# A two-resolution attention and its feed-forward layer: batch 0's mask and sums on TensorE, batch 1 in halves

## The chip, the core and the metric

The kernel runs on one NeuronCore of a Trainium2 chip. The core has five engines with instruction queues of their own: TensorE (PE, matmuls, with its weight loads shown as PEld), VectorE (DVE), ScalarE (ACT), GpSimd (POOL) and SyncE (SP), which here only issues transfers. TensorE writes to PSUM, eight banks of 128 x 512 fp32; DVE and ACT bring results from there to SBUF, POOL works in SBUF alone. Transfers are issued by SP and by POOL and run on 16 DMA engines. The metric is the time on the device in microseconds (us). Before the change it is 363.93, the median of 3 runs (363.8 to 364.75).

## The reference

For 8 batches of 8 heads with 576 tokens of 64 elements, attention is computed twice and added: on q, k, v averaged over groups of 4 tokens (144 x 144 scores per head), its result repeated 4 times; and on the full tokens, where a token sees only those less than 4 positions away. The result, 4608 tokens x 512, goes through a feed-forward layer with ELU.

```python
factor = 4
scale = 1.0 / np.sqrt(D)
q_d = q.reshape(B, H, Sd, factor, D).mean(axis=3)      # k_d, v_d alike
out_up = np.repeat(sm_attn(q_d, k_d, v_d), factor, axis=2)
mask = np.abs(pos[:, None] - pos[None, :]) < factor
scores = np.where(mask, scale * np.matmul(q, k.transpose(0, 1, 3, 2)), -1000000000.0)
attn = softmax(scores)
x = (out_up + np.matmul(attn, v)).transpose(0, 2, 1, 3).reshape(4608, 512)
h = x @ w_in                                           # 512 -> 2048
g = np.where(h > 0.0, h, np.exp(np.minimum(h, 0.0)) - 1.0)
return g @ w_out                                       # 2048 -> 512
```

## The kernel before, in words

**Attention.** A batch has four pairs of heads; a pair fills TensorE's 128 rows. For each pair q and k are loaded (96 tokens on the partitions, six columns of them), cast to fp16 (`cast`), transposed on TensorE by a matmul with an identity (`transposes`; the averages over four tokens come from a second matmul with the matrix BY6 for batches 0 and 1, whose tokens are loaded in another order, or from extra columns of ONE for the rest) and evicted to SBUF (`evq`, `evk`). `scores` multiplies, for each of six blocks of 96 queries, the 102 keys that can be in reach, and the averaged tokens beside them; ACT takes the exponential of each head; DVE multiplies the local part by the 0/1 tile MASK (line 644). `denominators` sums exponentials on TensorE (four pairs in four column groups of the array at once), DVE takes reciprocals, and these are spread over the head's 64 partitions: for batches 0 and 1 by TensorE with the constant SEL and a copy by ACT (`spr`, `evr`), for the others by two transfers through DRAM. `pool_v` averages v. `outputs` multiplies exponentials and v, DVE normalises (`normalize`, line 771, tile xn, three buffers), and an addition of the local and the repeated part writes the block of x, transposed, that the feed-forward layer reads (line 787, tile xt).

**Feed-forward.** Nine blocks of 512 tokens ("stages" 0 to 8). In a stage `mm1` does 16 groups of four matmuls with w_in (line 804), ACT takes exp, DVE min and the ELU's sum (lines 812 and 815); `mm2` does four results of 16 matmuls with w_out (line 827), each in four groups; ACT copies and SP stores. A batch has 576 tokens, so batch 0 fills the first block and 64 tokens of the second. Attention of later batches runs between the groups of earlier stages.

**What sets the order.** Nothing is issued in program order. Every step is an `Op` with an engine, an estimated length, a rank and the buffers it needs. `Plan.run` simulates engines and transfers with these estimates and, whenever an engine is free, starts the ready step of lowest rank; `emit` issues the steps in the order found, which each engine then keeps. Ranks are worked out from the numbers in PARAM. Before the first stage the planner fills PE's gaps up to a time FILL with matmuls on zeros (line 329, 221 of them, 17.3 us busy). Gates hold transfers back: `LGATE` makes loads of batch 1 wait for a named step by a small DVE memset into their buffer (line 879), `WGATE` orders weight transfers behind POOL's casts. Since SP issues in order, a gated load holds all that stand behind it. w_in comes in five transfers (bounds in WIC), w_out in four, all on POOL's queue.

**Constants.** DVE fills nine tiles (`fills`), POOL cuts the diagonals and bands with selects (`diagonals`, `masks`); transposes wait for the first, masks and denominators for both.

**Batch 0's end.** Each of four pairs is normalised; per pair, 512 of the 576 tokens are added for the first block by POOL (288) and DVE (224), and 64 by POOL for the second.

```python
    c_a = op("POOL", 2.0, -60, diagonals, after=[o_fill], name="diag")
    c_b = op("POOL", 1.9, -59, masks, after=[o_fill], name="masks")
            eng = "DVE" if b == 0 and g == 1 and t == 0 else "POOL"
        op("PE", 0.863, r, lambda: go(range(DMC)), reads=[x], writes=[h], after=[wi_ops[fc]], name=f"mm1_{t}_{fc}")
            need = [o for o in gt.writers if int(o.name.split("_")[1]) < 4 * part + 4]
            o.pre.add(wo_ops[part])
```

Of the kernel before, what the change touches and what calls it, by code (L numbers as in the profile page):

```python
# [31 lines left out]
DEN_GROUPS = {0: ((0, 1), (2, 3))}  # L32
# [3 lines left out]
LGATE = (None, "mask01", "mask02", "mask03", "recip02", "xn00", "xn01", "xn02", "xn03", "elu0_0", "elu0_2", "elu0_4", "elu0_8")  # L36
BY_PE = (0, 1)
V0 = ("DVE", "ACT")
WIC = (0, 256, 512, 1024, 1536, 2048)
# [30 lines left out]
class Plan:  # L70


    LAT = {"PE": 0.22, "ACT": 0.09, "DVE": 0.09, "POOL": 0.15}
# [60 lines left out]
    def run(self):  # L134
# [24 lines left out]
        busy = dict.fromkeys(ready, 0.0)  # L159
        events, now, order, lanes = [], 0.0, [], []  # L160
# [13 lines left out]
        while n < len(self.ops):  # L174
            for e, todo in ready.items():
# [36 lines left out]
                if o.nbytes:  # L212
                    if e == "SP":
                        lanes.append(o)
                    queues[e].append([o, o.nbytes / o.rate])
                    done = None
                else:
                    done = now + dur + (self.LAT[e] if o.lag is None else o.lag)
# [7 lines left out]
            then = min(events[0][0] if events else 1e9, land() if now >= 2.0 else max(land(), 2.0))  # L226
            if now >= 2.0:
                for e, f in shares().items():
                    x = queues[e][0]
                    x[1] -= (then - now) * f  # L230
                    if x[1] < 1e-6:
                        queues[e].pop(0)
                        heapq.heappush(events, (then + 1.5, x[0].i, x[0]))
            now = then
            self.filling = now < self.fill
            while events and events[0][0] <= now + 1e-9:
                _, _, o = heapq.heappop(events)
                if o is None:
                    continue
# [14 lines left out]
    def emit(self):  # L254
        for o in self.order:
# [8 lines left out]
PARAM = dict(M0=30, P=36.77, LAG=1.06, LEAD=53.49, GAP=7.69, SC=3.9, DEN=33.04, OUT=1.4, OUTG=1.98,  # L264
             LOAD=23.14, VLOAD=27.91, VCAST=36.99, warm=3.4, FILL=27.63, WI=-27.58, WO=38.12, WOG=2.24,
             OVER=1.0, LEAD1=57.82, GAP1=5.57, OUT1=32, VLOAD1=41.43, LOAD1=28.31, CC=-45.43, tv0=-26.96,
             C0=-7.99, SC0=2.71, OUTA=-25.9, OUTB=-21.42, DEN0=3.42, DENB=-28.86, SPA=-26.1, SPB=-20.87,
             V0=-46.5, G0=1, G1=2, G2=3, G3=3, G4=3, G5=8, G6=3, G7=13, G8=13, L0=2, L1=6, L2=0, L3=8,
             L4=0, LAG0=1.07, QG=2.08)
# [3 lines left out]
def kernel(  # L273
# [62 lines left out]
    def const(name, shape):  # L336
# [9 lines left out]
        "GAP": const("GAP", [QB, 41]),  # L346
        "SEL": const("SEL", [128, 640]),
# [4 lines left out]

    def fills():
        for t, x in (("ONE", 0.0), ("BY6", 0.25), ("VR", 0.25), ("MASK", 1.0), ("IND", 0.0), ("FIRST", 1.0), ("GAP", 0.0)):
            nc.vector.memset(C[t][:], x)  # L355
        nc.vector.memset(C["ONE"][:, QB:], 0.25)
        nc.vector.memset(C["VR"][:, 24:], 0.0)
        nc.vector.memset(C["IND"][:, 9:10], 1.0)
        nc.vector.memset(C["FIRST"][:, 1:10], 0.0)
        for i in range(3):  # L360
            nc.vector.memset(C["GAP"][32 * i : 32 * i + 24, 9:10], 1.0)
        for t in T["kt"]:
            nc.vector.memset(t[:, 0:3], 0.0)
            nc.vector.memset(t[:, S + 3 : S + 6], 0.0)
        for t in KD:
            nc.vector.memset(t[:], 0.0)

    o_fill = op("DVE", 1.6, -98, fills, name="fills")
# [9 lines left out]
    def diagonals():  # L378
        band(C["BY6"][:], [[1, NB], [-4, SD]], 6, 0, 3)
        nc.gpsimd.affine_select(  # L380
            out=C["ONE"][:, 0:QB], in_=C["ONE"][:, 0:QB], pattern=[[-1, QB]], compare_op=AB.not_equal, fill=1.0,
# [482 lines left out]
    for i in range(9):  # L864
        weights(i)
# [63 lines left out]
```

## Time and profile before

| what | before |
|---|---|
| median of 3 runs | 363.93 us (363.8 to 364.75) |
| the profiled execution: its time, its span | 364.62 us, 362.9 us |
| mean clock granted to TensorE | 0.984 |
| busy: PE, DVE, ACT, POOL | 347.5, 224.4, 211.5, 144.0 us |
| matmuls with w_in, with w_out (busy) | 141.2, 140.3 us |
| matmuls on zeros | 221, 17.3 us |
| moved by DMA | 48.89 MB, 135 GB/s in the mean |

Busy times say how long instructions of an engine were under way; a PE that is busy may run pipelined matmuls or small ones. What counts is where PE stands while something else ends last, and at which clock it runs. In the page's slices each digit is the busy share of a fortieth of the span, 9.07 us. In timelines the columns are start, length, engine, line, operation, output and inputs; in brackets the idle time before and what released the engine. A table of stretches gives for each engine its busy time and its number of instructions.

### The profile page before, as it was taken

How to read it: one execution, taken by the hardware profiler on the slowest of the kernel's cores; microseconds unless marked ns; L12 is line 12 of the kernel's file. 1: busy time of each engine (PE TensorE's matmuls, PEld its weight loads, DVE VectorE, ACT ScalarE, POOL GpSimd, SP SyncE). 2: the span in 40 equal slices, each digit the busy share in tenths (PEclk: the TensorE clock that was granted, in tenths of full speed). 3: DMA queues.
4: the chain of work that ended last, by engine and by line, in shares of the span. 5: the costliest groups of instructions: out<-in, count | busy, mean ns of one | idle time of the engine just before them, and what ended most of it. 6: DMA issues, size and time to landing. Idle time of an engine off the chain costs nothing.

```text
span 362.9 us, 8968 instructions
## 1 busy us (share of the span) xinstructions
PE 347.5 (96%) x3677; PEld 189.3 (52%) x3677; DVE 224.4 (62%) x410; ACT 211.5 (58%) x364; POOL 144.0 (40%) x226
## 2 busy tenths in 40 slices
PE   8995999999998998999999999999999999999995
PEld 7984554455454554554555455555554444444442
DVE  3658598336885597557755865398547667765510
ACT  2643696469865677557855785488557415544411
POOL 7645554277274544570557055634330160000000
PEclk9998799899999999999999999999999999999999
DMA  8999999999979799479746975103001311010021
GB/s 218 216 157 225 258 199 191 202 201 235 234 168 222 193 181 220 93 157 214 155 94 153 218 149 99 61 35 83 31 30 60 87 48 40 0 58 33 29 77 68
DMA packets 114366, 48.89 MB, mean 135 GB/s; under 512 B 100662, under 2 KB 108662, under 8 KB 114326
## 3 DMA queue, kind: packets, MB, share of 16 engines
q1 hardware_dynamic: 108038, 39.49, 52.3%
q0 software_dynamic: 6288, 8.84, 13.3%
q8 instruction: 28, 0.46, 0.6%
q14 instruction: 12, 0.10, 0.1%
HBM read 42.86 MB, written 9.66 MB: 145 GB/s over the span
## 4 chain that ended last, share of the span: by engine, by line
PE 78%; DVE 9%; ACT 6%; issue 2%; DMA 2%; POOL 2%; ACTq 0%; DVEq 0%; POOLq 0%
PE bank L827 32%; PE bank L804 27%; PE bank L548 4%; PE bank L620 3%; PE bank L748 3%; DVE e L812 3%; PE bank L329 3%; ACT e L810 2%; DVE gt L815 2%; PE bank L665 2%; ACT ex L637 2%; DVE ex L644 2%; DMA rcb<-rd 1%; PE bank L540 1%; PE bank L756 1%
## 5 line engine op out<-in xcount | busy, mean ns | idle before, releaser
L804 PE MATMUL bank<-xt,WI 128*128 128x512 f16 x576 | 141.2, 382 | 1.6 <-DVE gt L815 1.4
L827 PE MATMUL bank<-WO,gt 128*128 128x512 f16 x576 | 140.3, 381 | 1.9 <-DVE gt L815 1.9
L810 ACT ACTIVATE e<-bank 128x512 f16<-128x512 f32 x144 | 85.1, 603 | 49.1 <-PE bank L804 27.2
L815 DVE SCALAR_TENSOR_TENSOR gt<-bank,e 128x512 f16<-128x512 f32 x144 | 97.8, 688 | 4.9
L827 PEld LDWEIGHTS <-gt 128*128 128x128 f16 x576 | 54.0, 98 | 64.4 <-DVE gt L815 2.6
L804 PEld LDWEIGHTS <-WI 128*128 128x128 f16 x576 | 53.1, 98 | 64.0 <-issue 6.3
L812 DVE TENSOR_SCALAR e<-e 128x512 f16<-128x512 f16 x144 | 55.4, 386 | 39.6 <-ACT e L810 38.8
L516 POOL CAST c<-ld 96x768 f16<-96x768 f32 x60 | 50.6, 861 | 50.5 <-issue 25.7
L637 ACT ACTIVATE ex<-bank 102x864 f16<-102x864 f32 x64 | 53.4, 887 | 23.7 <-PE bank L628 23.5
L787 POOL TENSOR_TENSOR xt<-xn 128x288 f16<-128x288 f16 (+8 forms) x92 | 44.4, 514 | 54.1 <-DVE xn L771 54.0
L644 DVE TENSOR_TENSOR ex<-ex,MASK 102x1152 f16<-102x1152 f16 x32 | 28.6, 895 | 41.5 <-ACT ex L637 41.4
L842 ACT COPY os<-bank 128x512 f32<-128x512 f32 x36 | 21.3, 590 | 46.4 <-PE bank L827 43.4
L771 DVE TENSOR_TENSOR xn<-bank,rcb 128x720 f16<-128x720 f32 x32 | 27.8, 901 | 25.6 <-PE bank L756 23.8
L473 POOL CAST v<-v 102x768 f16<-102x768 f32 x32 | 27.5, 887 | 0.3 <-DMA v<-in_v_dram 0.3
L548 PEld LDWEIGHTS <-c 96*128 96x128 f16 x288 | 18.1, 97 | 8.0 <-issue 0.4
L563 ACT CAST qt<-bank 128x720 f16<-128x720 f32 x24 | 18.3, 761 | 4.2 <-PE bank L548 3.7
L548 PE MATMUL bank<-ONE,c 96*128 96x120 f16 x288 | 20.6, 216 | 0.0
L719 POOL DMA_DIRECT2D rd<-rc x6 | 3.5, 578 | 41.3 <-DVE rc L692 19.7
L329 PE MATMUL bank<-zero 128*128 128x128 f16 x221 | 17.3, 240 | 1.8 <-DVE ONE L355 1.1
L620 PEld LDWEIGHTS <-kt 64*102 64x102 f16 x384 | 11.7, 125 | 12.6 <-ACT e L810 4.7
L575 ACT CAST kt<-bank 128x576 f16<-128x576 f32 x24 | 15.6, 651 | 1.2 <-ACT qt L563 1.2
L329 PEld LDWEIGHTS <-zero 128*128 128x128 f16 x221 | 15.1, 109 | 2.4 <-DVE zero L332 1.1
(67 smaller groups left out, 228.6 us busy)
## 6 DMA issues: line engine op xcount, KB each, us to landing
ld<-in_q_dram SPq DMA_DIRECT2D x32, 288.0 KB, 5.2
ld<-in_k_dram SPq DMA_DIRECT2D x32, 288.0 KB, 5.4
out_dram<-os SPq DMA_DIRECT2D x36, 256.0 KB, 2.0
v<-in_v_dram SPq DMA_DIRECT2D x13, 672.0 KB, 8.8
rcb<-rd POOLq DMA_DIRECT2D x12, 360.0 KB, 5.6
WO<-in_moe_w_out_dram POOLq DMA_DIRECT2D x4, 512.0 KB, 9.1
WI<-in_moe_w_in_dram POOLq DMA_DIRECT2D x3, 512.0 KB, 11.3
v<-in_v_dram SPq DMA_DIRECT2D x3, 336.0 KB, 8.6
```

Source lines behind the costliest of these rows:

```text
L329: nc.tensor.matmul(PS[:, 7, 384:512], zero[:, 0:128], zero[:, 128:256], start=True, stop=True)
L516: f(out=at(y)[:], in_=at(x)[:].rearrange("p e c d -> p c e d"))
L548: nc.tensor.matmul(o, t[:, c, :, :], C["ONE"][:], start=True, stop=True)
L637: lambda e=e: nc.scalar.activation(out=at(x)[:, e], in_=two(sc[e], 0, KW, 0, HB + SD), func=AF.Exp, scale=SCALE),
L644: nc.vector.tensor_tensor(out=a, in0=a, in1=mk, op=AB.mult)
L771: lambda: nc.vector.tensor_tensor(out=at(w)[:], in0=two(z, 0, 128, 0, GW), in1=at(y)[:, j], op=AB.mult),
L787: (nc.vector if eng == "DVE" else nc.gpsimd).tensor_tensor(out=at(xt(t))[:, j, o : o + n - a], in0=ln, in1=gn, op=AB.add)
L804: nc.tensor.matmul(one(h, 0, 128, 0, TBLK), WI[:, dc, 128 * fc : 128 * fc + 128], at(x)[:, dc, :], start=(dc == 0), stop=(dc == DMC - 1),)
L810: op("ACT", 0.55, r, lambda: nc.scalar.activation(out=at(e)[:], in_=one(h, 0, 128, 0, TBLK), func=AF.Exp), reads=[h], writes=[e], name=f"e ...
L812: op("DVE", 0.42, r, lambda: nc.vector.tensor_scalar(out=at(e)[:], in0=at(e)[:], scalar1=1.0, scalar2=-1.0, op0=AB.min, op1=AB.add), reads ...
L815: op("DVE", 0.64, r, lambda: nc.vector.scalar_tensor_tensor(out=at(gt)[:, fc, :], in0=one(h, 0, 128, 0, TBLK), scalar=0.0, op0=AB.max, in1 ...
L827: nc.tensor.matmul(one(z, 0, 128, 0, DM), at(gt)[:, fc, 128 * tt : 128 * tt + 128], WO[:, fc, :], start=(fc == 0), stop=(fc == FCN - 1),)
```

## The change

Batch 0 changes in two ways, batch 1 in one, and the planner's estimates and numbers all change.

- **Mask.** For batch 0 the product with MASK on DVE goes. TensorE first writes a tile NEG (0 where a key is in reach, -30000 elsewhere) into the score banks, by four matmuls with an identity EYE per pair, and the scores accumulate on it.
- **Sum.** For batch 0's first block the additions by POOL and DVE go. TensorE adds the local and the repeated part with EYE in one PSUM bank per pair (four matmuls), and ACT copies the bank to xt.
- **Constants.** Each is made by a step of its own, in another order; MASK is cut for one block by POOL and copied to the others by DVE; the identity is EYE.
- **Batch 1.** Denominators and spreads are done for two pairs at a time, and the pooled v becomes a step of its own.
- **w_in** comes in four transfers of 512 columns; weight gates and load gates are other steps.
- **Engines of batch 0's casts and evictions** are set one by one: all four q casts and the third k cast on POOL, the other k casts on DVE; evictions of q on DVE but for the second pair, those of k on ACT for the first two pairs and on DVE for the others.
- The planner models transfers with other rates, starts and landings. Its order has 140 matmuls on zeros.

```diff
+MASK_BY_PE = (0,)
-DEN_GROUPS = {0: ((0, 1), (2, 3))}
+DEN_GROUPS = {0: ((0, 1), (2, 3)), 1: ((0, 1), (2, 3))}
...
-LGATE = (None, "mask01", "mask02", "mask03", "recip02", "xn00", "xn01", "xn02", "xn03", "elu0_0", "elu0_2", "elu0_4", "elu0_8")
+LGATE = (None, "recip00", "evv00", "recip00", "recip02", "xn00", "xn01", "xn02", "xn03", "elu0_0", "elu0_2", "elu0_4", "elu0_8")
-WIC = (0, 256, 512, 1024, 1536, 2048)
+WIC = (0, 512, 1024, 1536, 2048)
...
-             V0=-46.5, G0=1, G1=2, G2=3, G3=3, G4=3, G5=8, G6=3, G7=13, G8=13, L0=2, L1=6, L2=0, L3=8,
-             L4=0, LAG0=1.07, QG=2.08)
+             V0=-44.04, G0=1, G1=0, G2=4, G3=3, G4=12, G5=10, G6=13, G7=13, G8=13, L0=0, L1=1, L2=5, L3=10,
+             L4=2, LAG0=1.13, BY4=-31.8, TV1=4.97, C1=-16.44, e_x0=1, e_x1=1, e_x2=1, e_x3=1, e_cq0=1, e_cq1=1,
+             e_cq2=1, e_cq3=1, e_ck0=0, e_ck1=0, e_ck2=1, e_ck3=0, e_q0=0, e_q1=1, e_q2=0, e_q3=0, e_k0=1,
+             e_k1=1, e_k2=0, e_k3=0, QG=1.2)
...
+    c_six = op("POOL", 2.2, -60, sixths, name="sixths")
+    c_eye = op("POOL", 0.25, -59, eye, after=[o_clear], name="eye")
+    c_m1 = op("POOL", 0.75, -58, mask1, after=[o_clear], name="mask1")
+    c_m6 = op("DVE", 0.55, -57, mask6, after=[c_m1], name="mask6")
+    c_mask = op("POOL", 0.25, -56, edge, after=[c_m6], name="edge")
+    c_neg = op("DVE", 0.45, -54, lambda: nc.vector.tensor_scalar(
+        out=C["NEG"][:], in0=C["MASK"][:], scalar1=-1.0, scalar2=30000.0, op0=AB.add, op1=AB.mult), after=[c_mask], name="neg")
...
+            if hide:
+                for e in range(2):
+                    for g in range(2):
+                        nc.tensor.matmul(
+                            PS[0:KW, sc[e].slot[0] + g, 0:HB], C["EYE"][0:KW, 0:KW],
+                            C["NEG"][:, 3 * g : 3 * g + 3].rearrange("p c u -> p (c u)"), start=True, stop=False,
+                        )
...
-        op("DVE", 0.76, r + 0.6, mask, reads=[x], writes=[x], after=[c_b], name=f"mask{b}{j}")
+        if b not in MASK_BY_PE:
+            op("DVE", 0.76, r + 0.6, mask, reads=[x], writes=[x], after=[c_mask], name=f"mask{b}{j}")
...
+    def add_by_pe(j, r, w):
+        z, x = Buf("one"), xt(0)
+        def go():
+            for g, a, n in ((0, 0, HB), (1, HB, TBLK)):
+                ln = at(w)[:, g, 0 : n - a]
+                gn = at(w)[:, g, HB : HB + (n - a) // 4]
+                gn = bass.AP(tensor=gn.tensor, offset=gn.offset, ap=list(gn.ap) + [[0, 4]])
+                nc.tensor.matmul(one(z, 0, 128, a, n), C["EYE"][:], ln, start=True, stop=False)
+                nc.tensor.matmul(one(z, 0, 128, a, n), C["EYE"][:], gn, start=False, stop=True)
+        op("PE", 0.45, r + 0.3, go, reads=[w], writes=[z], after=[c_eye], name=f"sum0{j}")
+        eng = ("DVE", "ACT")[PARAM[f"e_x{j}"]]
...
+        if b == 0:
+            add_by_pe(j, r, w)
+            cuts = [TBLK, S]
...
-        if b == 0:
+        if b in DEN_GROUPS:
             yv, zv, w, tv = pool_v(b)
```

## The prediction, made before the changed kernel ran

> **What bounds the kernel now.** I read the slices of the page first, then the chain that ended last, then the engines stretch by stretch, then DVE's and PE's timelines around the places where PE stands. In the slices PE is 8 or 9 tenths busy everywhere except the fourth, and that is the only slice with a clock below 8:
>
> ```profile
> PE   8995999999998998999999999999999999999995
> POOL 7645554277274544570557055634330160000000
> PEclk9998799899999999999999999999999999999999
> DMA  8999999999979799479746975103001311010021
> ```
>
> From the first w_in matmul (37.36 us) to the last w_out matmul (end 358.82) PE has something to do nearly always, so the span is: the start of that matmul, PE's work behind it, PE's waits in that work, and 4.1 us for the last store. The chain that ended last passes to PE for good only after a DVE step:
>
> ```profile
> 31.24 3.28 DVE xt L787
> ...
> 35.26 0.90 DVE xn L771
> 37.56 1.71 PE bank L804 x4
> ```
>
> That step is an addition of two fp16 tiles that lasts 0.38 when POOL is idle and 3.35 while POOL runs five instructions back to back (31.68 to 34.26). DVE's timeline, start and length first:
>
> ```profile
> 27.80 1.88 DVE L771 TENSOR_TENSOR xn<-bank,rcb 128x720 f16<-128x720 f32 x2
> 29.60 0.38 DVE L787 TENSOR_TENSOR xt<-xn 128x224 f16<-128x224 f16 x1
> ...
> 31.17 3.35 DVE L787 TENSOR_TENSOR xt<-xn 128x224 f16<-128x224 f16 x1
> 34.44 1.71 DVE L771 TENSOR_TENSOR xn<-bank,rcb 128x720 f16<-128x720 f32 x2
> ```
>
> The normalisations behind it hold PSUM banks, so PE's next transpose waits 3.9, and the clock falls. The table of stretches (PE, its weight loads, DVE, ACT, POOL, then clock, DMA share, GB/s):
>
> ```profile
> 27.00:30.40 3.40, 3.31 (x99) 2.83 (x97) 2.78 (x4) 1.42 (x2) 0.24 (x1) 1.00 1.16 261
> 30.40:33.80 3.40, 1.89 (x30) 1.41 (x26) 2.75 (x3) 2.34 (x4) 3.39 (x7) 1.00 1.10 195
> 33.80:37.30 3.50, 1.10 (x12) 1.20 (x13) 3.50 (x7) 0.00 (x0) 2.35 (x5) 0.51 1.14 231
> 37.30:40.70 3.40, 3.40 (x26) 1.55 (x24) 0.74 (x3) 1.88 (x4) 1.82 (x3) 0.50 1.11 296
> ...
> 64.60:68.00 3.40, 2.51 (x30) 1.31 (x28) 0.00 (x0) 2.88 (x5) 0.00 (x0) 1.00 1.27 217
> 68.00:71.40 3.40, 3.40 (x46) 2.09 (x45) 1.72 (x2) 0.08 (x1) 1.03 (x2) 0.50 1.34 191
> ```
>
> Two stretches run at half clock. The second follows the spreads of batch 1's reciprocals, the second place where PE stands:
>
> ```profile
> 64.81 0.63 PE L707 MATMUL bank<-rc,SEL 32*128 32x144 f16 x12
> 66.14 0.47 PE L707 MATMUL bank<-rc,SEL 32*128 32x144 f16 x6 [0.70 <-ACT rcb L714]
> 66.80 0.47 PE L707 MATMUL bank<-rc,SEL 32*128 32x144 f16 x6 [0.19 <-ACT rcb L714]
> ```
>
> **The change part by part.** The sum is made against the profiled execution: 364.62 (span 362.9), 0.69 above the median of 363.93. I use the order in which the changed program issues on each engine, with lengths and starts from PE's, DVE's and POOL's timelines.
>
> *A. The start of the first w_in matmul, now 37.36.* Constants: POOL now makes all of them in 2.12 to 7.83, so the first k cast (7.79) and its transposes (8.66) wait. Changed, POOL runs the fill of BY6 (on DVE 0.78; POOL's own price is not in the trace, at most about twice that), its two selects 1.95, EYE 0.26, one block of MASK 0.49, VR 0.81, one edge 0.25, then the q cast 0.82; the k cast goes to DVE (0.56) behind NEG. The q transposes come 0.4 later than today's 6.22, the k transposes at about 7.4, 1.2 earlier. Each score block then carries four mask matmuls of 288 columns, 0.49 together (a 512-column matmul issues every 0.216), on a PE that ran 221 filler matmuls here; I take the last exp, now done at 24.11, as 1.0 earlier. The mask products go (last one 24.14 to 24.90), so the second denominators come 1.5 earlier, at 23.9, the outputs at 25.5, the first normalisation at 26.2 instead of 27.80. The second ends at 27.9, the third needs spread (0.42) and copy (0.76): 28.7 instead of 34.44, since no DVE addition lies before it. The fourth needs the first one's buffer (three of them), which POOL frees only after a cast of batch 1 (it waits for PE's transposes, about 29.6, and takes 0.82) and an add of 64 columns (0.24 to 0.5): 31.0, done 31.9. Then, per pair, TensorE's sum (1024 columns, 0.45), 0.2 to the reader, ACT's copy 0.59 (the 128x512 copy of L842), with an exp between: 33.9, first w_in matmul at 34.1. The w_in chunk that this matmul reads stands second in POOL's transfer queue behind one of the same 512 KB; today the first 1024 KB (256, 256 and 512) have landed at 27.7, so it lands near 28 and is no limit. The q block of batch 1's second pair is a risk: such loads took 7.5 us beside the weights (22.51 to 30.02), and one issued at 20 lands at 27 to 31. Five casts of batch 0 lie on POOL (four today) and DVE takes three evictions of q for three casts it gives up; both had gaps there (POOL 2.89 and 7.94, DVE 2.40 and 1.58), so I cost that at nothing, and if the gaps are gone it is part of the lower bound. I take 34.6: gain 2.8, bounds 0.9 (load and a blocked DVE step late) to 3.5.
>
> *B. Work moved ahead of it.* The scores of batch 1's first pair (0.64) and one transpose of its second (0.63) issue before the first w_in matmul instead of after it: gain 1.3.
>
> *C. The clock.* At 0.50 the first w_in group took 1.91 for 1.03, the scores 0.39 and the next group 0.27 too much: 1.5. Changed, PE works from 28.7 to 33.9 with small gaps: gain 1.3, bounds 0 (fewer fillers, 140 for 221) to 1.5.
>
> *D. Batch 1 in halves.* Denominators with the pooled v are 1.32 (62.52 to 63.84); two halves cost 0.88 each (18.43 to 19.31) and the pooled v 0.45: 0.9 more, and three more changes of array shape at 0.09. Loss 1.2, bounds 0.9 to 1.5.
>
> *E. The end of stage 0.* Now lost there: 0.3 before the last w_in group, 1.3 at the spreads, 1.6 by half clock, together 3.2. Changed, nothing stands between the second denominators and their spread: PE waits for DVE's reciprocal (1.05) behind the steps queued before it; the same way took 62.52 to 64.81, less 0.88 of own work: 1.4. The w_out chunk that the next matmul needs is issued second of its kind, behind casts of batch 1's v. SP issues in order, and that v stands behind a load now gated by the third w_in result (about 40.7, today 36.7), and SP has nothing else to issue while it waits; all loads of batch 2 stand behind too, and PE wants them only in the next stage. The v's first half lands at 48 to 50 (today 47.53), the chunk is issued at 50 to 51.3:
>
> ```profile
> DMA to landing us min/median/max: 7.3/9.1/10.1
> ```
>
> It lands at 57.3 to 61.4 and is wanted near 58.0 (34.6; the stage's work up to there, 23.3 today from 37.36 to 60.70, less 1.3 for B, 1.5 for C, 0.9 for a w_out group done in it today and 0.5 of waits, plus 1.6 for the first half of D with its spreads, 20.7; then 0.88, 1.4 and 0.43): 0 to 3.4, taken 0.8; the last chunk, two places of 4.3 behind it, 0 to 2, taken 0.5. A half-clock stretch after the wait: 0 to 1.7, taken 0.8. Together 3.5: loss 0.3, bounds gain 1.8, loss 5.3.
>
> *F. Later stages.* Ranks and gates move, the work is the same. DVE steps blocked by POOL cost PE 0.67, 1.91 and 1.29 at 96, 111 and 137; the worst is
>
> ```profile
> 104.58 4.35 DVE L644 TENSOR_TENSOR ex<-ex,MASK 102x1152 f16<-102x1152 f16 x1 [0.43 <-ACT ex L637]
> ```
>
> I leave it at nothing, bounds gain 3.0, loss 4.35 (another such block). From the denominators of batch 7 on both programs issue PE's work in the same order.
>
> Sum: 2.8 + 1.3 + 1.3 - 1.2 - 0.3 = 3.9; 364.62 - 3.9 = 360.7, less 0.69: **360.0**.
>
> In the row before 68.0 PE was busy 2.51 of 3.40 and the clock still halved. [...]
>
> The 3.35 addition lay under five POOL instructions. [...]
>
> **Rivals.** *w_out late (slower).* For: the load before it is gated later, and DMA took 13.1 for the slowest weight chunk. Against: no w_out chunk took over 10.1. Place: the first w_out matmul. At 51 + 13.1 = 64.1 it waits 6.1, and a half-clock stretch adds 1.7: 7.8 where the sum holds 2.1, so 365.7. It decides from a landing near 63.5 on. Chance 0.15.
>
> *The start hardly moves* (the mask and addition were covered anyway). For: 221 fillers say that PE was not the limit there, and loads share DMA. Against: the 3.35 step is on the chain. A 0.9 and C 0: 0.9 + 1.3 - 1.2 - 0.3 = 0.7, 363.2. Chance 0.12.
>
> *More blocked DVE steps,* because PE is ahead while POOL catches up on casts: one more of 4.35 leaves 364.4. Chance 0.08.
>
> *The later blocks vanish and E is only the 1.4:* 3.9 + 2.1 + 1.9 = 7.9, 356.0. Chance 0.08.
>
> **How the numbers follow.** The forecast runs from 357.2 (A 3.5, E the 1.4 alone) to 362.8 (A 0.9 and half a us of C or E) and has 0.57. A measurement of this kernel tells 0.3%, 1.1 us, from no change: 362.8 to 365.0 is the same. Faster: 0.57, 0.08 and a little of the second rival, 0.70. Same: most of the second and half of the third, 0.12. Slower: the first and the rest, 0.18. Leaving out 2 in 10 at most, the range is 356.3 to 365.2.
>
> **What would show it.** A: first w_in matmul (next to the sums, EYE as weights) near 34.6, no DVE addition of batch 0, no 3.9 wait of PE. C: clock 1.00 between 30 and 41. D: two blocks of 36 denominators matmuls for batch 1. E: one PE wait of about 1.4 ahead of a spread, then the first w_out matmul waiting or not for its chunk. Wrong would make it: a first w_in matmul after 36.5, a w_out landing after 63, or DVE mask products of over 3 us in batches 2 and 3.

## The result, and the profile after

The changed kernel is slower: 368.45 us (median of 4, 368.05 to 370.02) against 363.87, a ratio of 1.0129 with a 95% interval of 1.0095 to 1.0162. A second measurement gave 369.1 and 1.0185 (1.0151 to 1.0218). Single executions of one kernel lie up to 11 us apart here, and the slower ones have the lower mean clock (one variant below: 359.1 at 0.998, 366.3 at 0.979); the ratios leave out those more than 1.5% above the kernel's fastest, the medians do not.

The profiled execution took 370.02 (span 368.3), 5.4 more than the one before. Where the two stand at the same work, by the starts of matmul groups in both traces:

| work | before | changed | changed is |
|---|---|---|---|
| first w_in group | 37.36 | 36.47 | 0.9 ahead |
| 11th w_in group of stage 1 | 94.90 | 93.44 | 1.5 ahead |
| first w_out group of stage 1's third tile | 115.18 | 111.16 | 4.0 ahead |
| first w_in group of stage 2 | 122.02 | 122.67 | 0.6 behind |
| 11th w_in group of stage 2 | 135.89 | 140.61 | 4.7 behind |
| last w_out group | 357.80 | 362.39 | 4.6 behind |

The last store took 0.8 longer, which is the rest. So nearly all of the loss arises between 111 and 141 us, in stages 1 and 2, where the work is the same as before and only its order differs. From 141 us to the end the distance stays between 3.8 and 5.7, but for a few groups that the two programs place differently.

The slices of the page, the same rows as before the change (each digit is a fortieth of the span, 9.2 us):

```profile
PE   8989997999997889999999999999999999999994
...
POOL 7552164585274612592449134914250160000000
PEclk9996999999998989999999999999999999999998
DMA  8999199999999949979592976104100411010021
```

The 5 in PE's fourth slice is gone, but its clock there is 6 (28 to 37 us), and PE has weak slices at 55 to 64 and from 110 to 138; in the latter the clock is 8 twice. The DMA row has something that no step of mine asked about: the fifth slice, 37 to 46 us, is 1 where it was 9. The transfers on SP's queue show why, first before the change and then after it (start, length, queue, line, transfer):

```profile
36.69 0.31 SPq L442 DMA_DIRECT2D ld<-in_q_dram  x1
37.10 0.40 SPq L442 DMA_DIRECT2D ld<-in_k_dram  x1
37.55 5.73 SPq L470 DMA_DIRECT2D v<-in_v_dram  x2
```

```profile
43.30 0.31 SPq L487 DMA_DIRECT2D ld<-in_q_dram  x1
43.72 0.39 SPq L487 DMA_DIRECT2D ld<-in_k_dram  x1
44.16 3.65 SPq L515 DMA_DIRECT2D v<-in_v_dram  x2
```

These are the loads of batch 1's last pair. The gate on the third w_in result holds them until 43.3, SP has nothing else to issue, and the DMA engines stand: 54 GB/s in that slice against 258. That is 2.34 - 0.50 = 1.84 MB which must go later, 8 to 10 us at the 186 to 231 GB/s of the nine slices that follow. The last load of batch 2's q and k lands at 76.57 instead of 70.53, and the DMA row stays at 9 until 129 us, where before the change it had two 7s (100 to 109 and 118 to 127).

PE's timeline of the changed kernel, the lines with idle time (in brackets, with what ended it):

```profile
27.93 0.29 PE L808 MATMUL bank<-ex,vd 96*64 96x72 f16 x7 [1.48 <-issue]
...
59.62 0.61 PE L759 MATMUL bank<-rc,SEL 32*128 32x144 f16 x12 [1.17 <-DVE rc L744]
...
61.49 1.02 PE L898 MATMUL bank<-WO,gt 128*128 128x512 f16 x4 [1.25 <-DMA WO<-in_moe_w_out_dram]
...
115.54 0.45 PE L800 MATMUL bank<-ex,v 102*64 102x96 f16 x12 [2.50 <-DVE xn L841]
...
130.57 3.25 PE L875 MATMUL bank<-xt,WI 128*128 128x512 f16 x8 [2.79 <-DVE gt L886]
```

The chain that ended last names what lies behind the last two (start, length, what):

```profile
105.59 8.87 DMA rcb<-rd
114.64 0.76 issue
115.41 0.91 DVE xn L841
...
126.09 3.83 DVE e L883
```

A spread is one transfer to DRAM (`rd<-rc`) and two back, each for two pairs (`rcb<-rd`). At 105.59 the second one back is issued; it takes 8.87, DVE can't normalise before 114.6, and PE waits 2.50 for the bank. At 126.09 one DVE min, 0.29 where POOL is idle (124.57), takes 3.83: POOL runs two casts of batch 4 and the four casts of its v from 125.86 to 130.59 without a pause. The spread's late issue is in POOL's queue, before and after:

```profile
103.18 1.24 POOL L724 DMA_DIRECT2D rcb<-rd  x2 [1.77 <-ACT e L810]
104.42 1.60 POOL L516 CAST c<-ld 96x768 f16<-96x768 f32 x2
```

```profile
103.43 0.63 POOL L776 DMA_DIRECT2D rcb<-rd  x1 [4.23 <-ACT e L881]
104.05 1.60 POOL L518 CAST v<-v 102x768 f16<-102x768 f32 x2
105.59 0.62 POOL L776 DMA_DIRECT2D rcb<-rd  x1
```

In the new order two casts stand between the two transfers. Landing times of the three transfers, first before the change and then after it:

```profile
DMA to landing us min/median/max: 3.4/4.3/5.5
```

```profile
DMA to landing us min/median/max: 5.6/6.5/8.9
```

The one to DRAM (issued at 99.23 and 97.29) takes 5.6 instead of 3.4, the second one back is issued 2.16 instead of 0.62 behind the first, and it takes 8.9 instead of 5.5: 2.2, 1.5 and 3.4, together 7.1 from the first issue to the last landing. Most of that is slower transfers, not the order on POOL.

Each such place cost twice here. The table of stretches of the changed kernel (PE, its weight loads, DVE, ACT, POOL, then clock, DMA share, GB/s):

```profile
25.10:28.50 3.40, 1.92 (x86) 1.75 (x81) 2.75 (x5) 0.00 (x0) 0.00 (x0) 1.00 1.21 235
28.50:31.90 3.40, 2.82 (x34) 2.63 (x29) 0.91 (x1) 2.24 (x4) 0.93 (x2) 0.50 1.24 220
...
59.20:62.60 3.40, 1.72 (x19) 0.92 (x21) 1.95 (x4) 1.42 (x2) 2.43 (x4) 1.00 1.25 218
62.60:66.10 3.50, 3.50 (x13) 1.04 (x8) 0.00 (x0) 1.07 (x2) 0.00 (x0) 0.51 1.17 175
113.90:117.30 3.40, 1.52 (x42) 1.13 (x42) 2.54 (x3) 0.00 (x0) 1.72 (x4) 1.00 1.18 247
117.30:120.70 3.40, 3.40 (x9) 1.22 (x8) 0.91 (x1) 0.00 (x0) 3.40 (x7) 0.50 1.25 217
127.50:130.90 3.40, 0.61 (x4) 0.19 (x3) 3.40 (x3) 0.60 (x1) 3.10 (x4) 1.00 1.25 246
130.90:134.30 3.40, 3.40 (x20) 1.31 (x19) 2.09 (x5) 1.04 (x2) 0.00 (x0) 0.50 0.66 115
```

In this execution each of the four places is followed by a stretch at half clock. Between 111 and 135 us the two waits (2.6 and 2.9 above the usual distance of these groups) and the two stretches (2.1 and 1.6, summed in the same way) make 9.2. Before the change PE lost 0.67, 1.91 and 1.29 in this part, together 3.9, without a half-clock stretch (counted in the same way; the brackets have the idle time alone, and the 1.91 begins with a short wait at 109.92):

```profile
96.52 0.25 PE L665 MATMUL bank<-ex,FIRST 102*32 102x144 f16 x4 [0.60 <-ACT os L842]
...
111.60 0.39 PE L827 MATMUL bank<-WO,gt 128*128 128x512 f16 x1 [1.29 <-DVE gt L815]
...
138.03 1.02 PE L804 MATMUL bank<-xt,WI 128*128 128x512 f16 x4 [1.12 <-DVE gt L815]
```

The difference is 5.3. Between the table's second and last row it is 6.0 (1.45 ahead, 4.6 behind); the rest is short waits of the changed kernel at 154, 169 and 206 us (0.20, 0.63 and 0.53), less one of the kernel before at 291.

### The profile page after: what moved, and what is told of

It is laid out like the page before. It is cut to its first block, busy times and chain, and to the rows that moved or that the text cites. A ratio compares the mean times of both kernels' runs of the same rounds, so it can differ in the third digit from the quotient of the medians.

```text
span 368.3 us, 8875 instructions
## 1 busy us (share of the span) xinstructions
PE 350.2 (95%) x3628; PEld 188.9 (51%) x3628; DVE 215.6 (59%) x409; ACT 213.4 (58%) x366; POOL 143.0 (39%) x222
## 4 chain that ended last, share of the span: by engine, by line
PE 76%; DMA 10%; DVE 5%; ACT 3%; SPq 2%; issue 2%; POOL 1%; ACTq 0%; DVEq 0%
PE bank L898 32%; PE bank L875 28%; PE bank L593 3%; PE bank L674 3%; PE bank L800 2%; DVE e L883 2%; DMA rcb<-rd 2%; DMA WO<-in_moe_w_out_dram 2%; SPq L515 2%; DMA v<-in_v_dram 2%; DMA SEL<-selc 2%; PE bank L717 2%; DVE gt L886 2%; DMA ld<-in_q_dram 1%; ACT ex L692 1%
## 5 line engine op out<-in xcount | busy, mean ns | idle before, releaser
L898 PE MATMUL bank<-WO,gt 128*128 128x512 f16 x576 | 142.3, 386 | 1.5 <-DMA WO<-in_moe_w_out_dram 1.3
L561 POOL CAST c<-ld 96x768 f16<-96x768 f32 x61 | 52.5, 873 | 82.9 <-issue 52.7
L883 DVE TENSOR_SCALAR e<-e 128x512 f16<-128x512 f16 x144 | 51.9, 363 | 39.9 <-ACT e L881 39.5
L858 POOL TENSOR_TENSOR xt<-xn 128x288 f16<-128x288 f16 (+8 forms) x88 | 43.3, 520 | 36.0 <-DVE xn L841 36.0
L699 DVE TENSOR_TENSOR ex<-ex,MASK 102x1152 f16<-102x1152 f16 x28 | 24.9, 890 | 40.6 <-ACT ex L692 40.6
L674 PE MATMUL bank<-qt,kt 64*102 64x96 f16 x384 | 16.0, 218 | 0.0
L800 PE MATMUL bank<-ex,v 102*64 102x96 f16 x384 | 13.4, 208 | 2.7 <-DVE xn L841 2.7
L800 PEld LDWEIGHTS <-v 102*64 102x64 f16 x384 | 10.3, 109 | 8.7 <-issue 8.6
```

The source lines that it names most:

```text
L561: f(out=at(y)[:], in_=at(x)[:].rearrange("p e c d -> p c e d"))
L674: nc.tensor.matmul(PS[0:KW, sc[e].slot[0] + c // 3, QB * (c % 3) : QB * (c % 3) + QB], kt[p, QB * c : QB * c + KW], qt[p, qa : qa + QB], s ...
L800: nc.tensor.matmul(PS[64 * e : 64 * e + 64, z.slot[0] + c // 3, QB * (c % 3) : QB * (c % 3) + QB], v_[:, j, e, c, :], ex[:, e, c // 3, QB ...
L858: nc.gpsimd.tensor_tensor(out=at(xt(t))[:, j, o : o + n - a], in0=ln, in1=gn, op=AB.add)
L883: op("DVE", 0.42, r, lambda: nc.vector.tensor_scalar(out=at(e)[:], in0=at(e)[:], scalar1=1.0, scalar2=-1.0, op0=AB.min, op1=AB.add), reads ...
L898: nc.tensor.matmul(one(z, 0, 128, 0, DM), at(gt)[:, fc, 128 * tt : 128 * tt + 128], WO[:, fc, :], start=(fc == 0), stop=(fc == FCN - 1),)
```

## Experiments

Three theories, which do not exclude each other. **L**: the gate makes every load late. **O**: the order on POOL splits the spread. **B**: casts without a pause block the min. Against them **D**: the parts themselves (mask, sums, halves) cost it, and **S** for the start: the stop of 1.48 that ends at 27.93, and that no engine ended, is a stop for code. In the first edits, all marked with `plan.emit()`, the planner's order is kept and one thing is taken out of it.

**The gate gone.**

```diff
+    plan.order = [o for o in plan.order if o.name not in ("gload13q", "gload13k")]
     plan.emit()
```

> The changed kernel without the two memsets that hold the loads of batch 1's last pair until the third w_in result; every queue keeps its order. Theory L (late loads): with the gate, SP stands from 36 to 43 us and everything behind it (v of batch 1, all of batch 2, hence the loads of batches 3 and 4) runs 4 to 6 us later than before the change, back to back just when batch 2's reciprocals pass through DRAM. Then without the gate load13q is issued near 37, the second spread transfer of batch 2 lands near 110 instead of 114.5, the 2.6 us wait ahead of the second outputs of batch 2 and the half-clock stretch behind it go, and the kernel takes 363.5 to 365.5. Rival P (the plan): batch 2's denominators are put earlier and PE is ahead, so the spread is waited for however early the loads are; then the wait stays over 1.5 us and the time is 367 to 369. Rival D (the parts themselves: halves of batch 1, mask and sums on TensorE cost it) expects 368 to 369 as well, with the waits at 112 and 130 us changed or not.

Measured: 362.3, ratio 0.9953 (0.9923 to 0.9984). The loads are issued from 31.06 on, the second spread transfer of batch 2 lands at 109.02, PE waits for neither the w_out chunk nor the spread. Its page and its PE timeline:

```profile
DMA  8999999999999959958864974103011310010021
```

```profile
123.68 1.86 PE L875 MATMUL bank<-xt,WI 128*128 128x512 f16 x4 [2.92 <-DVE gt L886]
```

The hole at 40 us is filled, and the blocked min is as it was. L holds, even if it says nothing on B. The second transfer back still took 8.3 here; from the first issue to its landing it was 15.2 instead of 17.2, and PE lost another 0.9 at transposes ahead of the outputs.

**Three loads of batch 4 moved behind a store.**

```diff
+    late_ = [o for o in plan.order if o.name in ("load41k", "load42q", "load42k")]
+    plan.order = [o for o in plan.order if o not in late_]
+    i = [o.name for o in plan.order].index("st1_0") + 1
+    plan.order[i:i] = late_
     plan.emit()
```

> The changed kernel with three loads of batch 4 (k of the second pair, q and k of the third) moved in SP's queue behind the first store of stage 1; nothing else moves. Theory C (contention): the second spread transfer of batch 2 takes 8.9 us because these loads share the DMA engines with it; without them it takes 5 to 6 and lands near 111, the 2.6 us wait falls under 0.7, and with the half-clock stretch behind it 3 to 4.5 us are saved: 364 to 365.5. If the additions and casts on POOL then run earlier too, the 3.8 us DVE step at 126 us shrinks and the time is nearer 362.5. Rival (the spread is slow by itself, or waits on POOL): landing after 113, time 367.5 to 369.

Ratio 1.0006 (0.9963 to 1.0049), median 365.8. The transfer landed at 110.84, after 7.8 instead of 8.9; the wait ahead of the second outputs was gone, the min took 2.28. The loads beside it cost it something, but less than I thought: 7.8 is not the 5 to 6 of the theory.

**The casts of v apart.**

```diff
+    x4 = at(st[4])
+    for j, n in enumerate(("elu2_3", "elu2_4", "elu2_5", "elu2_6")):
+        c = [o for o in plan.order if o.name == f"vc4{j}"]
+        g = Op("DVE", 0.07, 0, lambda j=j: nc.vector.memset(x4[0:1, j, 0, 0, 0:1], 0.0), f"gvc4{j}")
+        plan.order.remove(c[0])
+        i = [o.name for o in plan.order].index(n) + 1
+        plan.order[i:i] = [g] + c
     plan.emit()
```

> The changed kernel with the four casts of batch 4's v on POOL each made to wait for one ELU of stage 2 (the third to the sixth behind it), so that they no longer follow two other casts without a pause. Theory B (blocked DVE step): the min of stage 2 that took 3.83 us then takes under 1.7 (two casts), PE's 2.95 us wait ahead of the fifth w_in group shrinks to under 1.2, and with the half-clock stretch behind it 2 to 3.5 us are saved: 365 to 366.5. Rival: the min waits for something else, keeps over 3 us, and the time stays within 367.5 to 369.

Ratio 0.9991 (0.9960 to 1.0021), 363.7, better than expected. DVE's timeline has that min at 0.74, PE's has no wait behind it, and the one ahead of the outputs is still there:

```profile
124.30 0.74 DVE L883 TENSOR_SCALAR e<-e 128x512 f16<-128x512 f16 x1 [0.29 <-ACT e L881]
```

```profile
113.75 0.45 PE L800 MATMUL bank<-ex,v 102*64 102x96 f16 x12 [2.19 <-DVE xn L841]
```

B is shown. In this profiled execution the prologue kept its full clock, and the first w_in matmul started at 33.28, so part of the surplus over the expectation is not the edit's.

**23 matmuls on zeros fewer.**

```diff
+    i = [o.name for o in plan.order].index("spr00")
+    k = [o.name for o in plan.order].index("out00")
+    plan.order = [o for n, o in enumerate(plan.order) if not (i < n < k and o.name == "fill")]
     plan.emit()
```

> The changed kernel without the last 23 of its 140 matmuls on zeros (between the first spread of batch 0 and its first outputs). Theory S (stall for code): PE's 1.48 us stop in the middle of the outputs of batch 0's last pair, which no engine ended, comes with an instruction packet that moves from 25.48 to 26.42 us; with 46 instructions fewer ahead of them the outputs run before PE needs that packet, the stop goes, the first w_in matmul starts 0.7 to 2 us earlier than 36.47 and the kernel takes 366.5 to 368. Rival: the stop stays at the same instruction or the half clock comes one window earlier because of the missing matmuls: 368 to 370.5.

Ratio 1.0006 (0.9964 to 1.0049), median 365.6, but the profiled execution is its slowest, with both later waits and half clock from 28.59 to 35.42. The stop left the outputs and came back, 1.21 long, at the first transposes of batch 1. It moves with the count of instructions, which speaks for S; that the start gains by it is not shown here. The median is 2.9 to 3.5 below those of the changed kernel, more than expected, and this trace can't show why.

**The changed kernel again.**

> The changed kernel itself, unaltered, beside the others on one chip, because single executions of one program spread more than I took from four of them. Theory L+B (late loads, blocked DVE step): median 366 to 369, the profile with a wait of 2 to 3.5 us ahead of the second outputs of batch 2 and one of near 3 ahead of the fifth w_in group of stage 2, as in the first profile. Rival (luck of the executions): median 363 to 365, so that the variants of the first four runs gained nothing against it.

369.1, ratio 1.0185 (1.0151 to 1.0218). Waits of 1.88 and 2.78 at the same two places, the min again 3.83. It is not luck.

**Gate gone and casts apart**, both edits above.

> The changed kernel without the gate of the third pair's loads, and with the casts of batch 4's v each behind an ELU: both edits that took one wait away each. Theory L+B: both waits are gone, also the half-clock stretch behind them, 357 to 360, under the kernel before by 1 to 1.8%. Rival (what is taken away here is lost elsewhere, as blocks that move to other DVE steps or as later waits): 361 to 364.

358.0, ratio 0.9898 (0.9855 to 0.9941). Neither wait is left, and PE's clock halves once instead of four times between the warm-up and the last store. L and B together account for the loss and for more than it. One blocked step is left in a later place: a mask product takes 3.25 at 139.69, under four casts on POOL, and PE waits 1.13 at 143.93.

**The parts undone one by one**, the order planned anew each time. The mask:

```diff
-MASK_BY_PE = (0,)
+MASK_BY_PE = ()
```

> The changed kernel with the mask of batch 0 as DVE's product again (the four mask matmuls of each pair gone, planned anew). The prediction's step A: the product was on the path and its removal brought the second denominators 1.5 forward, less the mask matmuls; so they come 1.0 to 1.5 later than in the changed kernel (23.1 to 23.7 us there), the first w_in matmul too, and the time rises by 1 to 1.5. Rival (the product was covered, or TensorE's 0.58 us per pair costs as much): the second denominators within 0.4 of 23.4, time unchanged within 1 us.

It got faster: 362.25, ratio 0.9946 (0.9909 to 0.9983). The second denominators came at 24.35, 0.8 to 1.2 later than in the two profiles of the changed kernel (23.52 and 23.18), so that much of step A is right. But the first w_in matmul came at 34.32, not later than theirs. And in the new order the two spread transfers follow one another, PE waits at most 0.15 ahead of the second outputs of batch 2, and no min of stage 2 is blocked. The sums:

```diff
-        if b == 0:
-            add_by_pe(j, r, w)
-            cuts = [TBLK, S]
...
+            eng = "DVE" if b == 0 and g == 1 and t == 0 else "POOL"
```

> The changed kernel with the sums of batch 0's first block as additions by POOL and DVE again (planned anew). Step A: the DVE addition is blocked by POOL's run of additions and casts, the normalisations behind it hold the banks, the first w_in matmul starts at 38 to 40 us, and the time rises by 2 to 4. Rival (the block belonged to the old order of casts): no DVE addition over 1 us, start within 1 us of the changed kernel's, time unchanged within 1 us.

362.1, ratio 0.9966 (0.9930 to 1.0001), start at 34.02; the wait for the spread is gone, one of 2.07 for a blocked min is still there. The additions on DVE, all four of them (shortest, median and longest in ns):

```profile
L857 DVE TENSOR_TENSOR xt<-xn x4: 384/864/872, 27.8 to 32.3; 128x224 f16<-128x224 f16 x4
```

The 3.35 that I built step A on belonged to the old order of POOL's casts; in the new order it is gone without TensorE's sums. The halves:

```diff
-DEN_GROUPS = {0: ((0, 1), (2, 3)), 1: ((0, 1), (2, 3))}
+DEN_GROUPS = {0: ((0, 1), (2, 3))}
...
-        return den_rank(b, j | 1) + 0.3 + 0.1 * j
+        return den_rank(b, 3) + 0.3 + 0.1 * j
```

> The changed kernel with batch 1's denominators and spreads in one step for all four pairs again (planned anew). Step D of the prediction: halves cost 1.2, so undoing them alone gives 367 to 368. Theory L+B+O (no part costs it, the order found with all of them does): in the new order both spread transfers of batch 2 are issued one behind the other, so at least the first of the two waits is gone, and the time is 361 to 365.

365.0, ratio 1.0017 (0.9982 to 1.0053). Any of the three undone, and the order planned anew, removes most of the loss. So D falls as the cause of the loss: no single part costs it, the order found for all three does. In all three the gate and the hole in the DMA row stay (88, 61 and 114 GB/s in the fifth slice), but PE hardly waits for the spread. So late loads alone don't make this loss: they make it where they meet a split spread.

**The spread in one piece.**

```diff
+    n = [o.name for o in plan.order]
+    plan.order.insert(n.index("spi20") + 1, plan.order.pop(n.index("spi21")))
     plan.emit()
```

> The changed kernel with the second spread transfer of batch 2 moved ahead of the two casts that stand between it and the first one in POOL's order; nothing else moves. Theory O (order on POOL): these casts cost the transfer 1.5 to 2.2 us of start (issues 2.15 apart here, 0.62 before the change), so it lands 1.5 to 2 earlier, the wait ahead of the second outputs of batch 2 falls from 2.0 to 2.6 to under 1, and without a stretch at half clock behind it the time is 365 to 367; the blocked DVE step of stage 2 stays. Rival C (the loads beside it alone): it lands within 1 us of where it landed, and the time stays 368 to 370.

365.3, ratio 1.0075 (1.0045 to 1.0106). POOL's queue and PE's two places:

```profile
101.93 1.24 POOL L776 DMA_DIRECT2D rcb<-rd  x2 [4.99 <-ACT kt L620]
```

```profile
111.63 0.45 PE L800 MATMUL bank<-ex,v 102*64 102x96 f16 x12 [0.23 <-DVE xn L841]
...
123.49 3.08 PE L875 MATMUL bank<-xt,WI 128*128 128x512 f16 x8 [2.12 <-DVE gt L886]
```

From the first issue to the last landing the spread takes 14.7 instead of 17.2; 1.5 of the difference is the order. O is shown beside L: earlier loads, fewer loads beside it or the transfers together, each of the three alone takes the wait away.

**Fewer instructions, TensorE as busy.**

```diff
+    def wide():
+        nc.tensor.matmul(PS[:, 7, 256:512], zero[:, 0:128], zero[:, 0:256], start=True, stop=True)
+    merged = []
+    for o in plan.order:
+        last = next((x for x in reversed(merged) if x.eng == "PE"), None)
+        if o.name == "fill" and last is not None and last.name == "fill" and last.fn is fill:
+            last.fn = wide
+        else:
+            merged.append(o)
+    plan.order = merged
     plan.emit()
```

> The changed kernel with its 140 matmuls on zeros merged in pairs (72 left, most of 256 columns instead of 128): TensorE is busy as long with 136 instructions fewer. Theory S (stall for code): the stop of 1.4 to 2.2 us inside the outputs of batch 0's last pair is gone, or lies where TensorE waits for something else; the first w_in matmul starts at 33.3 to 35.4 instead of 36.5 to 37.0 and the time falls by 1.5 to 3.5, to 365.5 to 367.5. Rival (it is a wait for data that the profile doesn't show): the stop stays in the outputs of the last pair, time 368 to 370.

366.0, ratio 1.0104 (1.0078 to 1.0130). The stop is gone, the clock stays, and the first w_in matmul starts at 32.56, 4.5 earlier than in the second run of the unaltered kernel. Not all of that is the stop: with the casts apart a stop of 0.74 was there, the clock stayed at full too, and the start was 33.28. The stretches of this kernel, and PE's later waits:

```profile
25.10:28.50 3.40, 2.58 (x69) 2.15 (x62) 2.97 (x6) 1.53 (x3) 0.00 (x0) 1.00 1.20 237
28.50:31.90 3.40, 3.25 (x44) 2.56 (x44) 0.96 (x2) 3.40 (x8) 2.61 (x6) 1.00 1.22 228
```

```profile
110.87 0.69 PE L800 MATMUL bank<-ex,v 102*64 102x96 f16 x12 [2.99 <-DVE xn L841]
...
126.63 3.23 PE L875 MATMUL bank<-xt,WI 128*128 128x512 f16 x8 [2.78 <-DVE gt L886]
```

Of 6.3 us that it is ahead of that run at 106, 1.6 are given back at the spread and in two half-clock stretches behind it; 4.7 reach the last matmul.

**The gate in the kernel before.**

```diff
-             V0=-46.5, G0=1, G1=2, G2=3, G3=3, G4=3, G5=8, G6=3, G7=13, G8=13, L0=2, L1=6, L2=0, L3=8,
+             V0=-46.5, G0=1, G1=2, G2=3, G3=3, G4=3, G5=8, G6=3, G7=13, G8=13, L0=2, L1=6, L2=0, L3=10,
```

> The kernel before with one number of the change: the loads of batch 1's last pair wait for the third w_in result (as in the changed kernel) instead of the fourth normalisation of batch 0. Theory L alone (late loads cost by themselves): loads of batches 2 to 4 run some 4 us later, batch 2's spread meets them, and it takes 365 to 368 where the kernel before takes 363 to 364. Theory O (late loads only cost together with the order on POOL that splits the spread): 362.5 to 364.5.

367.9, ratio 1.0160 (1.0117 to 1.0203): one number of the change, and the kernel before is as slow as the changed one. The DMA row has a hole in the same slice (88 GB/s). But the loss sits elsewhere than I expected: PE's timeline has 0.65 just ahead of batch 2's outputs, where the kernel before waits 1.29, and, in stage 0,

```profile
70.59 1.86 PE L827 MATMUL bank<-WO,gt 128*128 128x512 f16 x4 [3.94 <-DMA WO<-in_moe_w_out_dram]
```

This is the mechanism of the prediction's first rival, a w_out chunk issued behind casts of a v that the gate made late (it lands at 70.55), but in the other kernel.

**All edits together**: gate gone, spread in one piece, casts apart, matmuls on zeros merged.

> The changed kernel with all four edits that each took one thing away: no gate on the third pair's loads, the second spread transfer of batch 2 ahead of the casts, the casts of batch 4's v each behind an ELU, the matmuls on zeros merged in pairs. If the start's gain was only given back at the later waits, it now stays: first w_in matmul at 32.5 to 34, and 354 to 356.5, that is 2 to 4 under the 358.0 of the kernel with the gate gone and the casts spaced. Rival (the stage that follows takes it again, by blocked DVE steps in stage 0 or late chunks of weights): 357 to 359.

355.7 (354.01 to 357.42), ratio 0.9766 (0.9726 to 0.9807): the fastest here, 2.3% under the kernel before. First w_in matmul 32.72, no wait over 0.5 of PE from 100 to 130 us. On its page:

```profile
PE   8999998999999998999999999999999999999994
...
PEclk9999998999999999999999999999999999999999
DMA  8999999999999999896947892003100310000021
```

It is 2.3 under the median of the version that keeps the stop, whose first w_in matmul starts at 35.39, so the early start seems to keep its worth once the two waits are gone; the two differ in the spread's order too. The blocked mask product is here as well (3.41 at 137.34, PE waits 1.29).

**The parts, on this kernel.** Each of the three undone as above, with all edits of the fastest one. In these three the loads of batch 5's v came to stand ahead of some casts of batch 4's v, which therefore read tokens of batch 5; the amount of work is the same.

> c2_all with the mask of batch 0 on DVE. Step A: 1.0 to 1.5 more than c2_all, with second denominators later by as much. Rival (the mask on TensorE is worth nothing): within 0.8 of c2_all.

> c2_all with the sums of batch 0's first block on POOL and DVE. Step A: the addition is blocked again or PE's transposes wait, 2 to 4 more than c2_all. Rival (the block went with the old order of casts): no DVE addition over 1 us, within 0.8 of c2_all or below it, since PE is spared four times 0.45 us and ACT four copies.

> c2_all with batch 1's denominators and spreads in one step. Step D (halves cost 1.2): 0.9 to 1.5 less than c2_all. Rival (what halves cost in array time they save in waits at the end of stage 0): equal or up to 3 more than c2_all.

359.7, 359.0 and 359.4, ratios 0.9888 (0.9838 to 0.9938), 0.9852 (0.9808 to 0.9896) and 0.9871 (0.9825 to 0.9917). Two were run again with those loads behind the casts:

```diff
+    for name in ("vm52", "vm50"):
+        n = [o.name for o in plan.order]
+        i, k = n.index(name), n.index("vc43")
+        if i < k:
+            plan.order.insert(k, plan.order.pop(i))
```

> c2_whole with the loads of batch 5's v behind the casts of batch 4's v again. If the undone halves cost it (the whole block of denominators waits for the last pair, and the outputs of batch 1 with it), it stays at 358 to 360.5, against 355.7 of c2_all; if the order of loads and casts did, it comes down to 354.5 to 356.5, and step D's loss of 1.2 would be seen as a gain here.

> c2_mask with the loads of batch 5's v behind the casts of batch 4's v again. If the mask's product on DVE costs it, 357 to 360, with second denominators 1 to 1.4 us later than c2_all; if the order of loads and casts did, 355 to 356.5.

357.0, ratio 0.9826 (0.9791 to 0.9862), and 357.1, ratio 0.9847 (0.9802 to 0.9892). Undoing the halves costs 0.6%, undoing the mask 0.8%, that is 2 to 3 us by the ratios and 1.3 to 1.4 by the medians, with intervals that overlap that of the fastest kernel (0.9726 to 0.9807). Each of the two parts is worth something between nothing and 3 us here. With the mask on DVE the second denominators start at 23.89 instead of 23.04, but the first w_in matmul at 32.21 instead of 32.72; in the other traces of this kernel with a part undone it starts at 32.89 (mask) and 31.96 (sums). So neither of the two parts brings the start forward by more than 0.2 here. The new order of constants, casts and evictions is left as the reason, and no run takes that apart. What the sums on TensorE are worth in time stays open.

## Why the prediction was wrong

The forecast was 360.0, the result 368.45. Of the 9.3 us between the forecast's 3.9 gain and the 5.4 loss of the profiled execution, 2.5 arose before 95 us (1.9 in A, 0.6 in E; B, C and D together came out at the forecast 1.4) and 6.0 in step F; 0.8 is the last store. None of the three signs of being wrong came in the profiled execution: the first w_in matmul at 36.47, the chunk of w_out at 61.45, no mask product over 2.2. The loss lay outside all three.

- **F failed, through a sentence in E.** The words "all loads of batch 2 stand behind too, and PE wants them only in the next stage" gave the late loads no price. I saw the gate, its 4 us, and SP's empty queue, and asked only when the first user needs its data. But the DMA engines idled for 7 us, and the bytes went in later stages, where they met the spread. F put the later stages at nothing, and its bound of 4.35 (one more block) held one mechanism. There were two, a blocked min and a late spread, each with a half-clock stretch, and the later stages lost 6.0 net. Also, F counts the 0.67 at 96 among the blocked DVE steps; the profile puts that wait down to a copy of ACT.
- **A: the hand chain was right until 26 us, then not.** POOL's fill of BY6, whose price I had only bounded, took 0.81, near the 0.78 of DVE's. Second denominators 23.52 (23.9 forecast), outputs 24.82 (25.5), first normalisation 26.02 (26.2), second done at 27.75 (27.9). Then TensorE stopped for 1.48, the spreads came at 28.16, the clock halved at 28.53, the fourth normalisation came at 33.03 (31.0) and the first w_in matmul at 36.47 (34.6): gain 0.9 instead of 2.8. With a shorter stop and the full clock it is 33.28, without the stop 32.56, beyond my upper bound. Two reasons that I gave for the gain don't hold: the blocked addition is gone in the new order anyway, and on the kernel without the waits the start is at most 0.2 later with the mask or the sums undone.
- **B** is as forecast: scores and transpose stand ahead of the first w_in matmul.
- **C's sign failed.** The clock is 0.50 from 28.53 to 35.35: the cold stretch moved ahead with the work. Behind the start C's gain is there, the first w_in group takes 1.03 at full clock; it is paid ahead of the start, in A.
- **D's sign is not borne out.** On the kernel without the waits, undoing the halves makes it 1.3 to 2.2 slower by the middle values, not 1.2 faster; the intervals overlap, and what they save is not settled.
- **E was near in sum and terms:** 1.17 for the reciprocal (1.4 forecast), 1.25 for the w_out chunk, which landed at 61.45 (57.3 to 61.4 forecast; 0.8 and 0.5), and 1.6 for the half clock (0.8): 4.1 against 3.5.
- **Rivals.** "More blocked DVE steps" came true, in a min of stage 2, at 3.83; it cost PE 2.9 and 1.6 more by the clock, 4.5 where the rival has 4.35. Its price was about right, but the late spread cost as much again. "W_out late" did not happen here (61.45, where it decides from 63.5 on), but happened in the kernel before as soon as it had the gate.

Two rows that the prediction stood on have their like in the changed kernel. PE was busy 2.51 of 3.40 ahead of a half clock; here no idle time of PE is longer than 2.79, and four stretches followed at half clock. The addition of 3.35 lay under five POOL instructions; the min of 3.83 lay under six, of 0.8 each.

## What to carry to other kernels

When a change moves a gate, draw the transfer queue's timeline first: here a stretch in which the DMA engines idled was paid later, at a small transfer (in the kernel before, at a chunk of weights) that sat on the path when the bytes arrived. An early gain is only as good as the next wait whose end is set by something else, so price the waits behind it by what ends them. Where a planner orders everything, undoing one part proves little until the order's accidents are taken out: here every part undone alone looked like the culprit.

## What the hardware showed that I had not expected

**TensorE stops where it seems to run out of code.** In nine traces it stops behind the same instruction, the 13th matmul of the last pair's outputs, for 0.74 to 2.15 us. Each time a packet of 16384 bytes on the instruction queue (28 of them, 0.46 MB, in either profile) had begun 2.2 to 2.7 us before PE went on (25.47 and 27.93 in the changed kernel, 25.75 and 28.27 in its second run, 24.64 and 27.17 without the gate). From the packet's begin to the stop PE issued 81 matmuls and weight loads in 0.8 us, small ones of 72 to 96 columns. With 46 instructions fewer ahead the stop came at a later instruction, with 136 fewer it was gone. That the stop is for code is my reading of these two edits and of the packets. The profile names nothing that TensorE waits for there (`issue`), and in the changed kernel the packet itself was under way from 25.47 to 26.41, while the stop lasted from 26.46 to 27.93.

**The half clock came in stretches of 3.41 us, and the same instructions met them or not.** They lasted 3.41 or 6.82 (62.66 to 66.08, 28.53 to 35.35), and 10.24 once, with the sums undone. A row of 1.92 busy us was followed by half clock in the changed kernel, one of 2.51 before the change, and one of 2.58 (matmuls on zeros merged) was not; the busy time of a row alone did not tell. In the kernel with the casts apart, whose first 30 us are the changed kernel's own, the prologue stayed at full clock and the first w_in matmul started at 33.28 instead of 36.47 to 37.02 (its stop was shorter too, 0.74 instead of 1.48 and 2.15). That is 3 us of luck in one place.
